# A first product of 20 products instead of 21, with its two halves overlapped, and the sums of x moved to the second product

## The chip, the cores and the metric

The kernel runs on one core of one Trainium2 chip. The metric is the device time of one execution in microseconds. A core has a matrix engine (PE in the profile), VectorE (DVE), ScalarE (ACT), GpSimd (POOL) and SyncE (SP, which here only issues DMAs). Each works through its own instructions in order and waits on semaphores for the others.

## The reference

A short causal convolution over tokens (7 taps, softmax weights, one set for each of 8 heads), then a two-layer network with a GELU in the form h·sigmoid(1.702 h), all in float32:

```python
# x (8, 4096, 192), weight (8, 7)
w = softmax(weight)                        # over the 7 taps
out = np.einsum('hk,bskhg->bshg', w, x_unf)   # x_unf: x and its 6 predecessors
x = out.reshape(32768, 192)
h = x @ w_in                               # (192, 2048)
g = h * (1.0 / (1.0 + np.exp(-1.702 * h)))
return g @ w_out                           # (2048, 192)
```

## The kernel before

All tokens are done in 32 steps ("big" 0 to 31) of 1024 tokens each; tokens lie along the free axis, features along the partitions. Every step has a convolution, a first product (w_in, and GELU on the way out of PSUM) and a second product (w_out). Step 0 is special (`first_step`), for the weights are still being unpacked then; the steady loop over `big` 1 to 31 stands at the end of the kernel function.

**First product.** The 192 features are 3 blocks of 64 (c = 0, 1, 2) and the tokens 2 blocks (n), so that x has six blocks; w_in has 4 by 3 blocks for each of two halves of its columns (v = 0, 1). The plain way takes 24 block products for each v. The kernel forms sums of blocks of w_in once (`SUMS_W`), and in each step sums of blocks of x (`SUMS_C`, eight of them), and takes 21 products of sums (`TERMS`, pairs of a sum of w_in and a sum of x), which it adds and subtracts into the eight outputs. A product (`product1`) is two matmuls of 64 rows, one for each row half of PE, and each writes one of the two PSUM banks of its slot; in float32 each matmul shows as two records, so a product is four records of 64 x 512. There are 4 pairs of banks: `slots[0]` to `slots[2]` and `sums`. `hidden(big, v, ...)` lists the order of a v half by hand: `pe` issues products, `copy2` (line 647, ACT) saves a pair of banks in a `room` place (k15 to k20), `sum2` (line 651, VectorE) adds or subtracts banks and places, `gelu` (lines 632 and 636, ACT) writes the rows of g. Between them `work` issues the convolution of block 1 (VectorE, `conv`), `taps_at` issues taps of the other blocks (ACT, `tap`), and `early` four groups of sums of the second product.

A product needs the same rows of x on both row halves, so each block and each sum is copied across the halves by DMA (`cross`, SP). `conv_t` has three parts: the own blocks and sums of even steps, the crossed ones, and the own ones of odd steps.

**Convolution.** Blocks 0 and 2 are made by taps: ACT multiplies by one weight (line 516) into a spare place, and either a DMA that accumulates (line 530, block 0, a small tree of sums) or GpSimd (line 518, block 2) adds up. Block 1 is made by VectorE, seven instructions (lines 502 and 504). The sums of x come from GpSimd (`sums_c`, lines 391 and 393; by VectorE in step 1), in the first product, through `prepare`.

**Second product.** Five by five blocks of g and w_out are again combined: `PLAN` is a list, written out, of main products (`main`), side products (`side`, on a fourth column strip of PE), sums of g (`sum`, VectorE, 128 x 1024), sums by an accumulating DMA (`acc`, issued by POOL), `seed` (ACT copies between places), `join` (VectorE), output transposes (`turn`) and stores. `("go", n)` issues n groups of four matmuls, three of the main product and one of the side; there are 78 groups of 0.433 us. A place of g is a `spot`, numbered 0 to 20; `("sum", 14, 14, "-", 18)` writes spot 14. Five sums (`EARLY_G`) are made by VectorE or DMA in the first product already. Spots that are no longer needed serve as places of the taps (`TAP_SPOTS`).

The engines are in order, and the program order is that of the lists (`manual_schedule`): an instruction that waits holds up all that stands behind it on its engine.

Of the kernel before, what the change touches and what calls it, by code (L numbers as in the profile page):

```python
# [8 lines left out]
F32 = mybir.dt.float32  # L9
# [6 lines left out]
def kernel(  # L16
# [8 lines left out]

# [41 lines left out]
    def load_x(big, ns=range(2)):  # L87
# [20 lines left out]
        [psum.tile([P, TOK], F32, name=f"slot{i}{h}") for h in range(2)] for i in range(3)  # L108
    ]
    sums = [psum.tile([P, TOK], F32, name=f"sums{h}") for h in range(2)]  # L110
# [17 lines left out]
    k15, k19, k20, k18, k16 = (room[:, i, :].rearrange("p (h n) -> p h n", h=2) for i in range(5))  # L128
# [17 lines left out]
    KEPT_LATE, TAP_SPOTS = 3, {0: (13, 16, 15), 2: (14, 17, 18), 3: (15, 16, 19)}  # L146

    def kept(i):
# [7 lines left out]
    NB = 13  # L156
    C11, C12, C21, C22, C31, C32, V2, V3, V4, V5, V6, V7, V8, V1 = range(NB + 1)
    conv_t = consts.tile([P, 3, NB, T], F32)
    SUMS_C = [
        (V1, C31, "-", C11),  # L160
        (V2, V1, "-", C32),
        (V3, C12, "+", V2),
        (V4, C22, "+", V2),
        (V5, C21, "-", V4),
        (V6, C11, "-", V5),
        (V7, C22, "-", C21),
        (V8, C32, "-", C22),
    ]

    def place(big, b):  # L170

        if b == V1:
            return V8 if big % 2 else C31
        return C31 if b == V8 and big % 2 else b

    def own(big):
        return conv_t[:, big % 2 * 2, :, :]
# [3 lines left out]
    NA = 21  # L181
    w_in_s = consts.tile([P, NA, UW], F32)
    SUMS_W = [
        (12, 10, "n", 11),
        (13, 12, "-", 2),
        (14, 3, "-", 12),
        (12, 1, "-", 13),
        (15, 4, "+", 13),
        (16, 3, "+", 5),
        (17, 2, "+", 5),  # L190
        (18, 0, "+", 3),
        (19, 6, "+", 8),
        (20, 19, "+", 10),
        (4, 4, "n", 16),
        (5, 2, "+", 11),
        (0, 0, "+", 2),
        (10, 7, "-", 10),
        (7, 7, "+", 19),
        (8, 8, "-", 11),
        (11, 9, "+", 11),  # L200
        (11, 11, "-", 19),
        (9, 9, "-", 3),
        (3, 3, "0", 3),
    ]

    TERMS = [
        (14, V2), (10, C21), (20, V5), (6, V3), (19, V6), (0, C11), (17, C32), (5, V8), (4, V7), (8, V1), (12, C22),
        (9, C12), (13, V4), (3, V3), (15, C22), (16, V6), (2, V1), (1, C21), (11, C11), (7, V7), (18, C12),
    ]

# [34 lines left out]
    assert PIECE == CW * D and 3 * PIECE <= NB * T and 3 * PIECE <= 2 * NJ * XW and 3 * PIECE <= FORMS * NG * HD  # L247
# [221 lines left out]
    def transpose_x(big, c, n=None):  # L469
# [14 lines left out]
        0: [conv_t[:, i, b : b + 2, :] for i in (1, 2) for b in (V2, V4, V6)],  # L484
# [23 lines left out]
    DMA_TAPS = (0,)  # L508
    TREE = {2: [(1, 2)], 4: [(3, 4)], 6: [(5, 6), (0, 1), (3, 5), (0, 3)]}
    TREE_1 = {2: [(1, 2)], 4: [(3, 4), (0, 1)], 6: [(5, 6), (0, 3), (0, 5)]}  # L510

    def tap(big, c, k):

        dst = own(big)[:, 2 * c : 2 * c + 2, :]
        home = tap_home(big, c, k) if k else dst
        act.mul(home, conv_src(big, c, k), cw[:, c, k : k + 1])  # L516
        if k and c not in DMA_TAPS and big > 1:
            nc.gpsimd.tensor_add(dst, dst, home)  # L518
            return
        homes = [dst] + [tap_home(big, c, i) for i in range(1, K)]  # L520
        for a, b in (TREE if big > 1 else TREE_1).get(k, ()):
            tree.append((homes[a], homes[b]))
        end_taps(2 if big == 2 and k == K - 1 else 0)

    tree = []

    def end_taps(left=0):
        while len(tree) > left:
            out, src = tree.pop(0)
            nc.gpsimd.dma_start(out=out, in_=src, accum_op=ALU.add)  # L530

    def sums_c(big, i):
        add_up(
            lambda j: own(big)[:, place(big, j), :],
            *SUMS_C[i],
            eng=vec if big == 1 else nc.gpsimd,
        )

    def cross(big, b0, b1):
        for o in range(2):  # L540
            nc.sync.dma_start(
                out=conv_t[halves[1 - o], 1, b0:b1, :], in_=own(big)[halves[o], b0:b1, :]
            )

    def copy_over(b):

        for o in range(2):
            act.copy(conv_t[halves[1 - o], 1, b, :], own(0)[halves[o], b, :])
# [3 lines left out]
    waiting = {True: [], False: []}  # L552
    given = {True: 0, False: -1}
    pieces = []

    def cross_now(early, big, b0, b1):
        if early or big == 1:
            cross(big, b0, b1)
        else:
            pieces.extend((big, b, min(b + 3, b1)) for b in range(b0, b1, 3))  # L560
# [5 lines left out]
    def cross_when(early, *what):  # L566
        if given[early] < what[0] - 1:
            waiting[early].append(what)
        else:
            cross_now(early, *what)  # L570

    def give(early, big):
        given[early] = big
        for what in waiting[early]:
            cross_now(early, *what)
        waiting[early].clear()

    def prepare(big):

        v1 = place(big, V1)  # L580
        def convs(*cs):
            for c in cs:
                for k in range(K):
                    yield "", 0.76 if k else 0.48, lambda c=c, k=k: conv(big, c, k)

        cost = 0.34 if big == 1 else 0.0
        yield from convs(1)
        yield f"conv {big}", 0.0, lambda: None
        yield f"done {big}", 0.0, lambda: need(f"taps {big}")
        yield "", cost, lambda: sums_c(big, 0)  # L590
        yield f"first {big}", 0.0, lambda: cross_when(True, big, v1, v1 + 1)
        yield "", 0.0, lambda: cross_when(False, big, 0, C31)
        for i in range(1, len(SUMS_C)):
            yield "", cost, lambda i=i: sums_c(big, i)
        rest = (C31, V8) if big % 2 else (C31 + 1, NB)
        yield f"all {big}", 0.0, lambda: cross_when(False, big, *rest)

    def prepare_taps(big):

        for c in (0, 2):  # L600
            for k in range(K):
                yield "", 1.0, lambda c=c, k=k: tap(big, c, k)
        yield f"taps {big}", 0.0, lambda: None

    def product1(slot, a, b, big, v, first=False):
        pair = conv_t[:, big % 2 : big % 2 + 2, place(big, b), :]
        for h in range(2):

            src = pair[halves[h], :, :] if h == big % 2 else pair[halves[h], ::-1, :]
# [9 lines left out]
    def terms(big, v, slot, *ts, first=False):  # L619
        for t in ts:  # L620
            product1(slot, *TERMS[t], big, v, first)
            first = False

    ALL = slice(0, TOK)

    def gelu(b, u, v, src):
# [3 lines left out]
        if isinstance(src, list):  # L630
            for h in range(2):
                act.activation(  # L632
                    dst[:, :, h, :], src[h].rearrange("p (o t) -> p o t", o=2), AF.Gelu_apprx_sigmoid
                )
        else:
# [3 lines left out]
                AF.Gelu_apprx_sigmoid,  # L639
            )  # L640
# [4 lines left out]
    def copy2(dst, src):  # L645
        for h in range(2):
            act.copy(bank(dst, h), bank(src, h))  # L647
# [10 lines left out]
    def hidden(big, v, x, z, y, sums, work, fetch, last=lambda: None):  # L658

        def pe(slot, *ts, first=False):
            terms(big, v, slot, *ts, first=first)

        def taps_at(n):
            for _ in range(0 if v else n):
                next_tap()

        def early(i):
            for item in (EARLY_G if big > 1 else EARLY_G_1)[i] if v else ():  # L670
                sum_g(*item)


        if v:
            pe(z, 7, first=True)
            give(True, big)
        if v:
            pe(sums, 12)
            copy2(k15, sums)
            pe(x, 5, 17)  # L680
        else:
            pe(x, 5)
            pe(sums, 12)
            copy2(k15, sums)
            pe(x, 17)
            taps_at(1)
        gelu(B11, 0, v, x)
        if not v:
            pe(z, 7, first=True)
        pe(sums, 0)  # L690
        copy2(k16, sums)
        taps_at(2)
        last()
        def turn_next():
            if big + 2 < N_BIG:
                need(f"done {big + 1}")
                turn_x(big + 2)

        early(0)
        if not v:  # L700
            work(2.0 if big > 1 else 1.6)
        elif big == 1:
            work(3.2)

        pe(y, 6, 14, first=True)
        sum2(vec.tensor_sub, x, z, k15)
        early(1)
        if not v or big == 1:
            work(1.6 if big > 1 else 1.2)
        pe(sums, 13)  # L710
        copy2(k19, sums)
        pe(x, 2)
        copy2(k18, x)
        taps_at(2)
        pe(z, 11)
        pe(sums, 20, 10)
        sum2(vec.tensor_sub, k15, y, k19)
        gelu(B12, 0, v, sums)
        pe(x, 4)
        copy2(k20, x)  # L720
        sum2(vec.tensor_sub, k19, z, k19)
        early(2)
        if not v or big == 1:
            work(1.1)
        gelu(B22, 1, v, k19)
        gelu(B22, 0, v, k15)
        taps_at(2)
# [565 lines left out]
```

## Time and profile before

| | |
|---|---|
| time, median of 3 runs | 2295.59 us (2294.99 to 2295.61) |
| profiled execution, span | 2294.0 us |
| busy: PE, VectorE, ACT, GpSimd | 2271.9, 1939.3, 1563.3, 843.7 us |
| matmuls of line 610, 64 x 512: records | 5400 (3740 into `slot`, 1660 into `sums`) |
| stages: first product of step 1 | 106.8 to 153.2 us |
| stages: step 12 | 887.5 to 923.8 (first), to 957.6 (second) |

The profile is of one execution. Its span runs from the first to the last instruction. A line of a group names the source line, the engine and the operation, what is written and read, the shape and the count, then the busy time, the mean length in ns, and the engine's idle time just before with what ended it. A window line gives for a stretch of time how long each engine was busy, and the number of instructions. A line that ends in `[0.40 <-PE sums L610]` says that the engine idled 0.40 us before it and what it waited for.

### The profile page before, as it was taken

What the parts mean: (1) busy time and instruction counts of PE and PEld (TensorE: products, weight loads), DVE (VectorE), ACT (ScalarE), POOL (GpSimd) and SP (SyncE); (2) the same over time, 40 slices, a digit from 0 to 9 for tenths busy, and PEclk for the clock granted to TensorE, in tenths of its full rate; (3) what the DMA queues carried; (4) which work ended last, traced back from release to release, by engine and by line L of the source; (5) the groups of instructions that cost most, each with busy time, mean ns of one, the idle gap of its engine ahead of it and who ended that gap; (6) DMA issues with size and microseconds to landing.
All of it is one profiled execution on the core that took longest, in us unless ns stands there. A gap on an engine that the chain in (4) does not pass through costs nothing.

```text
span 2294.0 us, 60960 instructions
## 1 busy us (share of the span) xinstructions
PE 2271.9 (99%) x25214; PEld 1206.9 (53%) x25214; DVE 1939.3 (85%) x2791; ACT 1563.3 (68%) x2968; POOL 843.7 (37%) x837
## 2 busy tenths in 40 slices
PE   9889999999999999999999999999999999999998
PEld 5355555555555555555555555555555555555556
DVE  8778888888888888888888888888888888888877
ACT  7567666677666776666776667776667766677754
POOL 1444433344424434333444234343334442344400
PEclk9899999999999999999999999999999999999999
DMA  8885666665666656666656656566666566564443
GB/s 196 149 158 117 117 125 136 128 125 113 126 133 125 138 113 117 125 136 128 127 113 127 134 123 139 113 115 125 139 127 128 113 127 135 122 140 86 91 98 70
DMA packets 270660, 286.56 MB, mean 125 GB/s; under 512 B 118064, under 2 KB 206128, under 8 KB 270256
## 3 DMA queue, kind: packets, MB, share of 16 engines
q0 software_dynamic: 58080, 151.48, 36.8%
q1 hardware_dynamic: 210656, 130.80, 25.4%
q8 instruction: 199, 3.26, 0.6%
q10 hardware_dynamic: 1648, 0.39, 0.1%
q14 instruction: 77, 0.63, 0.1%
HBM read 53.15 MB, written 25.17 MB: 34 GB/s over the span
## 4 chain that ended last, share of the span: by engine, by line
PE 94%; DMA 3%; DVE 1%; ACT 1%; POOL 0%; issue 0%; SPq 0%; POOLq 0%; ACTq 0%; DVEq 0%
PE slot L610 33%; PE slot L985 33%; PE sums L610 15%; PE sums L985 12%; DMA w_form<-w_form 1%; DMA g<-g 1%; DMA conv_t<-conv_t 0%; POOL w_form L437 0%; DMA conv_t<-w_form 0%; DMA w_out_s<-w_form 0%; DMA osbs<-in_moe_w_out_dram 0%; DVE xt L473 0%; DMA xin<-in_x_dram 0%; DVE conv_t L504 0%; ACT conv_t L1090 0%
## 5 line engine op out<-in xcount | busy, mean ns | idle before, releaser
L610 PE MATMUL slot<-conv_t,w_in_s 64*128 64x512 f32 x3740 | 861.6, 591 | 6.3 <-ACT room L647 6.0
L985 PE MATMUL slot<-g,w_form 128*32 128x256 f32 x7024 | 710.3, 379 | 0.0
L610 PEld LDWEIGHTS slot<-conv_t,w_in_s 64*128 64x128 f32 x3740 | 374.6, 187 | 432.7 <-issue 352.3
L393 DVE TENSOR_TENSOR g<-g 128x1024 f32<-128x1024 f32 x372 | 450.2, 1237 | 3.2
L985 PEld LDWEIGHTS slot<-g,w_form 128*32 128x32 f32 x7024 | 373.5, 110 | 119.7
L610 PE MATMUL sums<-conv_t,w_in_s 64*128 64x512 f32 x1660 | 407.9, 591 | 0.9 <-ACT room L647 0.6
L636 ACT ACTIVATE g<-room 128x1024 f32<-128x1024 f32 x310 | 325.7, 1077 | 67.1 <-DVE room L651 67.1
L1010 ACT COPY room<-slot 32x256 f32<-32x256 f32 x434 | 159.3, 367 | 310.4 <-PE slot L985 309.2
L985 PE MATMUL sums<-g,w_form 128*32 128x256 f32 x2648 | 368.8, 379 | 0.0
L985 PE MATMUL slot<-g,w_out_s 128*32 128x256 f32 x4080 | 318.8, 380 | 0.0
L961 POOL DMA_DIRECT2D g<-g x124 | 106.3, 858 | 499.2 <-PE sums L985 165.9
L610 PEld LDWEIGHTS sums<-conv_t,w_in_s 64*128 64x128 f32 x1660 | 172.0, 187 | 188.2 <-issue 141.4
L518 POOL TENSOR_TENSOR conv_t<-conv_t,g 128x512 f32<-128x512 f32 x180 | 260.5, 1447 | 14.3 <-POOL conv_t L518 3.0
L530 POOL DMA_DIRECT2D g<-g x120 | 104.3, 885 | 429.9 <-PE sums L985 119.5
L647 ACT COPY room<-slot 128x512 f32<-128x512 f32 x434 | 231.5, 601 | 40.8 <-PE slot L610 40.8
L516 ACT ACTIVATE g<-xt,cw 128x512 f32<-128x512 f32 x360 | 248.5, 730 | 2.2
L985 PEld LDWEIGHTS slot<-g,w_out_s 128*32 128x32 f32 x4080 | 164.7, 110 | 131.7 <-ACT g L632 22.7
L632 ACT ACTIVATE g<-slot 128x512 f32<-128x512 f32 x334 | 180.7, 598 | 45.1 <-PE slot L610 23.5
L985 PEld LDWEIGHTS sums<-g,w_form 128*32 128x32 f32 x2648 | 177.9, 110 | 36.7
L504 DVE SCALAR_TENSOR_TENSOR conv_t<-xt,cw,conv_t 128x512 f32<-128x512 f32 (+1 forms) x198 | 189.1, 955 | 4.6
L393 POOL TENSOR_TENSOR conv_t<-conv_t 128x256 f32<-128x256 f32 x180 | 182.2, 1026 | 9.4
L1010 ACT COPY room<-sums 32x256 f32<-32x256 f32 x217 | 79.6, 367 | 145.2 <-PE sums L985 142.5
(203 smaller groups left out, 2914.9 us busy)
## 6 DMA issues: line engine op xcount, KB each, us to landing
g<-g POOLq DMA_DIRECT2D x124, 512.0 KB, 5.6
xin<-in_x_dram SPq DMA_DIRECT2D x240, 180.0 KB, 4.4
conv_t<-conv_t SPq DMA_DIRECT2D x180, 192.0 KB, 3.2
g<-g POOLq DMA_DIRECT2D x120, 256.0 KB, 3.8
out_dram<-osbs SPq DMA_DIRECT2D x186, 128.0 KB, 5.0
g<-room POOLq DMA_DIRECT2D x31, 512.0 KB, 5.3
conv_t<-g POOLq DMA_DIRECT2D x60, 256.0 KB, 4.6
g<-osbs POOLq DMA_DIRECT2D x30, 512.0 KB, 4.7
```

Source lines behind the costliest of these rows:

```text
L393: eng.tensor_sub(v(dst), v(a), v(b))
L504: vec.scalar_tensor_tensor(out=dst, in0=src, scalar=tap, in1=dst, op0=ALU.mult, op1=ALU.add)
L516: act.mul(home, conv_src(big, c, k), cw[:, c, k : k + 1])
L518: nc.gpsimd.tensor_add(dst, dst, home)
L530: nc.gpsimd.dma_start(out=out, in_=src, accum_op=ALU.add)
L610: nc.tensor.matmul(slot[h], w_in_s[halves[h], a, v * P : (v + 1) * P], src, start=first, stop=True, skip_group_check=True,)
L632: act.activation(dst[:, :, h, :], src[h].rearrange("p (o t) -> p o t", o=2), AF.Gelu_apprx_sigmoid)
L636: act.activation(dst.rearrange("p o h t -> p h o t"), src.rearrange("p h (o t) -> p h o t", o=2), AF.Gelu_apprx_sigmoid,)
L647: act.copy(bank(dst, h), bank(src, h))
L961: nc.gpsimd.dma_start(out=spot(dst), in_=spot(a), accum_op=ALU.add)
L985: nc.tensor.matmul(dst, w, t, start=first, stop=last, skip_group_check=True)
L1010: act.copy(to, d)
```

## The change

- `SUMS_C` has eleven sums of five of the six blocks of x (block 4 is only in sums), `SUMS_W` 23 sums, `TERMS` 20 products. `slots` has all four pairs of banks, and `sums` is one of them.
- `FIRST` replaces the hand-written order: one list for a v half. Names a0 to a9 are pairs of banks, given out from a list `free` when first named and given back after the last use (`COUNT`); k0 to k6 are places in `room` (`ROOM_OF`). The first number of an item tells whose it is: 0 of this v half; 1 and 2 of the next one, so that eight of the 20 products of a half are done ahead. In v = 0 they are those of v = 1. In v = 1 the opening product (mark 2, the only one on block 2 of the six of x) is that of the next step; the items of mark 1 are put on `later`: the copies go out in the second product (`seeds_ahead`, at `final`), the rest at the start of the next first product (`rest_ahead`).
- `FILL` hangs other work on places of that list: twelve GpSimd adds of the convolution, three transposes of x, the early sums of g. `work` and taps are left there for step 1 alone (`FILL_1`).
- `conv_t` has the own blocks twice (by step), but one place for the eleven sums, one for their crossed copies and one for the crossed blocks, except the crossed block of the opening product, which has two. So the sums of the next step can be made only when the first product has been read: `vsum` items in `PLAN` (GpSimd), with `cross` items behind.
- Conv block 1 (c = 1) of steps from 3 on is made by taps on ACT too; GpSimd adds up blocks 1 and 2, and block 0 stays with the DMA tree (`tree` items). All 21 taps stand in `PLAN` (7 did before, at most one between two `go`; now up to four).

In the text, "P19" is the product of entry 19 of `TERMS`, counted from 0.

```diff
-    k15, k19, k20, k18, k16 = (room[:, i, :].rearrange("p (h n) -> p h n", h=2) for i in range(5))
+    rooms = [room[:, i, :].rearrange("p (h n) -> p h n", h=2) for i in range(5)]
...
-    KEPT_LATE, TAP_SPOTS = 3, {0: (13, 16, 15), 2: (14, 17, 18), 3: (15, 16, 19)}
+    KEPT_LATE, TAP_SPOTS = 3, {0: (11, 10, 16), 1: (17, 14, 20), 2: (15, 13, 9), 3: (15, 16, 19)}
...
-    conv_t = consts.tile([P, 3, NB, T], F32)
+    conv_t = consts.tile([P, 2 * NBLK + 2 * NV + len(REST) + 2, T], F32)
     SUMS_C = [
...
+        (6, 0, "-", 4), (7, 6, "-", 5), (8, 1, "+", 7), (9, 3, "+", 8), (10, 0, "-", 7), (11, 9, "-", 6),
+        (12, 2, "-", 10), (13, 2, "-", 4), (14, 13, "+", 11), (15, 0, "+", 14), (16, 14, "-", 1),
     ]
...
+    TERMS = [
+        (13, 9), (6, 14), (9, 0), (14, 5), (11, 6), (7, 2), (1, 3), (15, 3), (0, 0), (4, 16), (16, 8), (10, 2),
+        (17, 15), (18, 7), (2, 11), (8, 12), (3, 1), (12, 1), (5, 10), (19, 13),
+    ]
...
         if k and c not in DMA_TAPS and big > 1:
-            nc.gpsimd.tensor_add(dst, dst, home)
+            adds.append((dst, home))
+            if big == 2:
+                next_add()
             return
...
-    def hidden(big, v, x, z, y, sums, work, fetch, last=lambda: None):
...
+    FIRST = [
+        (0, "gelu", 2, 1, "a0", 1), (0, "prod", 14, "a1"), (0, "copy", "k0", "a2", 1),
+        (0, "sum", "a3", "a4", "-", "k1"), (0, "prod", 17, "a3"), (0, "sum", "a5", "k1", "-", "a1"),
+        (0, "prod", 3, "a4"), (0, "gelu", 3, 1, "a3", 1), (0, "prod", 16, "a5"), (0, "sum", "a6", "k0", "-", "a4"),
+        (0, "prod", 1, "a1"), (0, "gelu", 1, 0, "a5", 1), (0, "prod", 15, "a6"), (0, "prod", 7, "a4"),
+        (0, "copy", "a7", "a6", 1), (0, "gelu", 1, 1, "a4", 1), (0, "prod", 19, "a6"),
+        (0, "sum", "a8", "a1", "-", "k2"), (0, "prod", 5, "a7"), (0, "prod", 12, "a8"), (0, "copy", "k3", "a6", 1),
+        (0, "sum", "k4", "a8", "+", "k3"), (0, "gelu", 0, 1, "a7", 1), (2, "prod", 11, "a0"),
+        (1, "copy", "a2", "a0", 1), (0, "prod", 9, "a1"), (1, "prod", 0, "a2"), (1, "prod", 4, "a0"),
+        (0, "gelu", 2, 0, "k4", 1), (1, "copy", "k2", "a2", 1), (0, "prod", 8, "a8"),
+        (0, "sum", "a1", "a1", "+", "k3"), (1, "prod", 10, "a2"), (1, "copy", "k6", "a0", 1),
+        (0, "gelu", 0, 0, "a8", 1), (0, "sum", "k5", "a1", "-", "k0"), (1, "sum", "a4", "a2", "-", "k6"),
+        (1, "prod", 6, "a9"), (1, "prod", 2, "a0"), (1, "prod", 13, "a4"), (0, "gelu", 3, 0, "k5", -1),
+        (1, "copy", "k1", "a9", 1), (1, "prod", 18, "a2"),
+    ]
...
+    FILL = [
+        {
+            1: (("add", 4), ("add", 4), ("add", 4)), 9: (("turn", 0),), 15: (("turn", 1),), 21: (("turn", 2),),
+        },
+        {
+            3: (("g", 0),), 12: (("g", 1),), 17: (("g", 2),), 18: (("g", 3),), 31: (("g", 4),), 36: (("g", 5),),
+        },
+    ]
...
+    def hidden(big, v, now, nxt):
+
+        for i, (ahead, *item) in enumerate(FIRST):
+            for what in (FILL if big > 1 else FILL_1)[v].get(i, ()):
+                fill(big, *what)
+            if not ahead:
+                do(big, v, now, *item)
+            elif v == 0:
+                do(big, 1, nxt, *item)
+            elif nxt and ahead == 2:
+                do(big + 1, 0, nxt, *item)
+            elif nxt:
+                later.append(item)
...
     PLAN = [
...
+        ("side", 13, 16, "k0"), ("main", 1, 5, "p2", 1), ("vsum",), ("cross",), ("go", 3), ("vsum",), ("go", 1),
+        ("sum", 14, 14, "-", 18), ("main", 16, 10, "p3", 0), ("go", 2), ("sum", 7, 8, "-", 7), ("tap",), ("go", 1),
+        ("go", 1), ("main", 0, 14, "p0", 1), ("cross",), ("go", 1), ("sum", 5, 11, "-", 19), ("go", 1),
...
+        ("vsum",), ("go", 1), ("sum", 6, 8, "-", 6), ("go", 1), ("main", 5, 8, "p1", 0), ("go", 1),
+        ("sum", 4, 5, "-", 10), ("tap",), ("go", 1), ("seed", "k2", "p2", 1), ("tap",), ("go", 2),
+        ("sum", 0, 0, "+", 5), ("main", 14, 2, "p2", 0), ("go", 1), ("vsum",), ("go", 1), ("acc", 15, 4), ("go", 1),
+        ("join", "k3", "p1", "+", "k0"), ("vsum",), ("go", 1), ("sum", 11, 7, "+", 11), ("side", 11, 17, "k0"),
...
     for big in range(1, N_BIG):
         more = big + 1 < N_BIG
...
+        rest_ahead(big, half)
+        other = begin_half()
+        hidden(big, 0, half, other)
+        half = begin_half() if more else None
+        hidden(big, 1, other, half)
         if more:
-            need(f"all {big + 1}")
+            need(f"done {big + 1}")
+            cross_blocks(big + 1)
+            begin_sums(big + 1)
```

New functions that these call: `do` runs one item of `FIRST` (a product, a pair of copies, a pair of sums, a GELU); `begin_half` makes an empty table of names; `next_sum` issues one sum of x on GpSimd and, when a group of two or three is complete, puts its crossing on the list that `cross` takes from; `add_taps` issues one DMA of the tree; `next_add` issues one GpSimd add of the convolution.

More of the change, by code (lines that the diff above doesn't have):

```diff
@@ L183 @@
     SUMS_W = [
[L184 to L202, printed above, removed]
@@ L547, in copy_over @@
         for o in range(2):
[L548 to L560, printed above, removed]
+            act.copy(conv_t[halves[1 - o], cross_of(0, b), :], own(0)[halves[o], b, :])
+    pieces, sums_left = [], []
+    LAST_AT = {s[0]: i for i, s in enumerate(SUMS_C)}
+    ENDS = (NBLK, NBLK + 3, NBLK + 6, NB - 2, NB)
+    GROUPS = [range(*ends) for ends in zip(ENDS, ENDS[1:])]
     def cross_piece():
@@ new lines, in begin_sums, with done @@
+    def begin_sums(big):
+        sums_left.extend((big, i) for i in range(len(SUMS_C)))
+    def prepare(big):
+        for k in range(K if big < 3 else 0):
+            yield "", 0.76 if k else 0.48, lambda k=k: conv(big, 1, k)
+        yield f"conv {big}", 0.0, lambda: None
+        def done():
+            need(f"taps {big}")
+            while adds:
+                next_add()
+            if OPEN_SUM:
+                sums_c(big, *OPEN_SUM)
+            cross(big, OPEN, OPEN + 1)
+        yield f"done {big}", 0.0, done
@@ L617, in product1, with gelu @@
             )
[L619 to L622, printed above, removed]
     ALL = slice(0, TOK)
-    def gelu(b, u, v, src):
+    def gelu(b, u, v, src, sign=1):
         m, n = divmod(b, 2)
@@ new lines, with seeds_ahead, rest_ahead, plain @@
+    later = []
+    def seeds_ahead(big, half):
+        while later and later[0][0] == "copy":
+            dst = later[0][1]
+            if dst[0] == "a" and dst not in half[0] and not free:
+                return
+            do(big, 0, half, *later.pop(0))
+    def rest_ahead(big, half):
+        while later:
+            do(big, 0, half, *later.pop(0))
+    def plain(u, m, n, v, slot, ks=range(NC), first=0):
+        for k in ks:
+            product1(slot, NC * (2 * u + m) + k, 2 * k + n, 0, v, k == first)
@@ new lines, in fill @@
+    def fill(big, kind, *args):
+        if kind == "work":
+            work(*args)
+        elif kind == "tap":
+            next_tap()
+        elif kind == "add":
+            for _ in range(*args):
+                next_add()
+        elif kind == "turn":
+            need(f"done {big + 1}")
+            if big + 2 < N_BIG:
+                transpose_x(big + 2, *args)
+                if args[0] == NC - 1 and big + 3 < N_BIG:
+                    load_x(big + 3)
+        else:
+            sum_g(*(EARLY_G if big > 1 else EARLY_G_1)[args[0]])
@@ L1260, with final @@
             begin(big + 2)
-        second(big, x, y, sums, lambda: copy2(sums, z) if more else None, not more)
-        x, z = z, x
+        bx, bs, by = (free.pop(0) for _ in range(3))
+        def final():
+            free.append(bs)
+            if more:
+                seeds_ahead(big + 1, half)
+        second(big, bx, bs, by, final, not more)
+        free += [bx, by]
 _INS = ['x', 'weight', 'moe_w_in', 'moe_w_out']
```

362 lines of the change are left out of this document (174 added, 188 removed), and 56 rows, old and new, of tables (PLAN, SUMS_W).

## The prediction

> **What bounds the kernel now.** I read the busy times of the page first, then its chain of work that ended last, by engine.
>
> ```profile
> PE 2271.9 (99%) x25214; PEld 1206.9 (53%) x25214; DVE 1939.3 (85%) x2791; ACT 1563.3 (68%) x2968; POOL 843.7 (37%) x837
> ...
> PE 94%; DMA 3%; DVE 1%; ACT 1%; POOL 0%; issue 0%; SPq 0%; POOLq 0%; ACTq 0%; DVEq 0%
> ```
>
> The matmul engine is the chain. Next come sums over windows: one step of the steady loop, cut where the matmuls change from line 610 (first product) to line 985 (second product), then the second product cut once more at 20 us.
>
> ```profile
> core 0: us, PE busy (x) PEld busy (x) DVE busy (x) ACT busy (x) POOL busy (x), PEclk, DMA share, GB/s
> 887.54:923.79 36.25, 36.25 (x172) 16.70 (x168) 29.90 (x41) 30.39 (x51) 19.54 (x17) 1.00 0.59 117
> 923.79:957.60 33.81, 33.81 (x626) 20.17 (x625) 30.06 (x44) 18.20 (x42) 7.74 (x9) 1.00 0.67 135
> ...
> 923.79:943.79 20.00, 20.00 (x374) 12.10 (x376) 19.30 (x22) 8.81 (x23) 4.29 (x5) 1.00 0.88 183
> 943.79:957.60 13.81, 13.81 (x260) 8.07 (x252) 10.75 (x23) 9.39 (x19) 3.45 (x4) 1.00 0.37 66
> ```
>
> PE has no gap in the step, at full granted clock: 36.25 + 33.81 = 70.06 us. A matmul removed is time gained, and every new wait of PE is time lost. The third row shows the neighbour with least room: in the first 20 us of the second product VectorE is busy for 19.30. It works there through the 17 sums that PLAN interleaves with the matmuls that read them. Last the timeline of that step, for the prices (start, length, what, x how many), with two lines from 112 us, when PE comes out of a wait:
>
> ```profile
> 906.53 1.02 PE L610 MATMUL sums<-conv_t,w_in_s 64*128 64x512 f32 x4
> 907.39 1.88 PE L610 MATMUL slot<-conv_t,w_in_s 64*128 64x512 f32 x8
> 907.59 1.07 ACT L647 COPY room<-sums 128x512 f32<-128x512 f32 x2 [0.40 <-PE sums L610]
> ...
> 910.60 2.40 POOL L393 TENSOR_TENSOR conv_t<-conv_t 128x256 f32<-128x256 f32 x2
> 911.19 1.22 DVE L393 TENSOR_TENSOR osbs<-g 128x1024 f32<-128x1024 f32 x1
> 912.51 1.56 DVE L393 TENSOR_TENSOR osbs<-osbs,g 128x1024 f32<-128x1024 f32 x1
> ...
> 919.67 1.28 DVE L651 TENSOR_TENSOR room<-room,sums 128x512 f32<-128x512 f32 x2 [2.07 <-PE sums L610]
> ...
> 925.10 2.35 DVE L393 TENSOR_TENSOR g<-g 128x1024 f32<-128x1024 f32 x2
> ...
> 112.07 0.59 PE L610 MATMUL slot<-conv_t,w_in_s 64*128 64x512 f32 x1
> 112.12 0.59 PE L610 MATMUL sums<-conv_t,w_in_s 64*128 64x512 f32 x1
> ```
>
> To be seen: one product of the first kind is 4 records and 0.86 us, start to start (906.53 to 907.39). Its reader on ACT starts 0.20 us after that (907.59), and two copies of a bank each take 1.07. VectorE's pair of bank sums takes 1.28. A 1024-wide sum of VectorE takes 1.22, but 1.56 when GpSimd sums beside it: 0.35 more. At 112 us the two row halves of PE (one bank each) run out of step by 0.06 us, a new product beginning on one half while the other ends the old one.
>
> **The product removed.** Each of 31 steps has two v halves, so 62 products fall away: 62 x 0.86 = 53.2 us, or 1.72 a step. Left are 40 products, 34.32 us a step.
>
> **The new order of the first product.** Before, two products at least lie between a reader of a bank pair and the next product into that pair. After, in several places only one does: P15, copy a7<-a6, P7, P19 into a6; P11, copy a2<-a0, P9, P0 into a2 (for v=1, inside v=0); P0, copy k2, P4, P10 into a2 at the start of a step. The copies of the two banks end 0.20 + 0.59 = 0.79 and 0.20 + 1.07 = 1.27 us after the product; PE starts some 0.15 us later (my estimate: at 906.25 a weight load follows the copy that frees its bank by 0.05, and the first matmul of a step takes 693 ns against 589). Cover is 0.86. If the row halves may run out of step, as at 112 us, each waits for its own bank: 0.79 + 0.15 - 0.86 = 0.08, the second half staying 0.43 to 0.48 behind. If the pair goes as one, 1.27 + 0.15 - 0.86 = 0.56. A fourth place, the chain gelu(1,1), sum a8, P12, is late by about 0.1. I followed the list of FIRST down with these prices (ACT 0.48 a bank start to start, VectorE 0.60): waits of 0.09 to 0.14 at six or seven places, plus 0.43 of offset that is paid when the second product needs all rows, make 1.2 us a step; with pairs as one, 2.9. Least is the offset alone, 0.4. I take 1.2, since the 112 us lines show halves apart. Behind each such wait stands everything on PE, which is in order.
>
> By load, ACT has 28 bank copies and 24 bank gelus at 0.48 and four wide gelus at 0.96: 28.8 us of 34.3; VectorE 32 bank sums at 0.60, five 1024-wide at 1.13 and three transposes at 0.68: 26.9. Neither becomes the bound there.
>
> **VectorE's late start in the second product.** Its last work in the first product now hangs on P9: sum a1, sum k5, early sum 5, then PLAN's first sum (spot 14). P9 ends 1.29 us before the end (P8's 0.86 and the 0.43 of offset); 0.26 + 1.2 + 1.2 + 1.13 later is 2.5 us into the second product, against 1.31 before (925.10). Spot 14 is read after 8 of 78 groups of four matmuls, at 8 x 0.433 = 3.47; the sum ends at 3.72, so PE waits 0.4 with its answer time. Lateness against before: 1.2.
>
> **Sums of x moved beside VectorE's queue.** Eleven sums a step on GpSimd (eight before) leave the first product; nine stand in the first 45 of 78 groups. Two run before VectorE's first sum; seven meet it where it has no gap: 7 x 0.35 = 2.45 us. The first sums are needed early: in the trace of before, those of spots 8, 13, 6 and 15 end 1.0, 1.7, 1.5 and 1.2 us ahead of their matmuls, and VectorE idles once, 0.46 us, before 13. At spot 15 the lateness is 1.2 + 2.45 - 0.46 = 3.2 against 1.2: PE has lost 2.0 us by then, the 0.4 included. Least: the meetings cost nothing and only the 0.4 stays. Most: a whole 0.73 of GpSimd (its length alone) each, 7 x 0.73 = 5.1, so 4.6. I take 2.0, by the 1.56 row. Queued behind are the joins and out turns on VectorE, and POOL's accumulating DMAs, whose readers are 9 us or more away.
>
> The Trainium skill (SBUF — State Buffer, Who interferes with whom) says that a VectorE instruction with two SBUF inputs contends with a GpSimd one that reads SBUF, and that the loser blocks fully, for the whole instruction. The trace agrees that it costs, but with 0.35, not 0.73; by the rule at its worst the sum would take the 4.6.
>
> **Conv block 1 (c = 1) and the rest: nothing.** VectorE loses seven conv instructions a step (six at 0.99 on the group row of line 504, one at 0.44), which lay beside PE. ACT gains 14 taps in the second product, 14 x 0.62 = 8.7 on 18.2 busy of 33.8; side copies wait behind at most four taps, 2.5 us, where their banks come round after 8 groups, 3.5 us: if that cover failed, up to 1 us a step. GpSimd's twelve adds at 1.45 start near the first product and end 17.4 us later; gelu(0,1) of v=0 needs the sixth, at 8.7, some 6 us ahead. SP issues 4 more crossings a step, each landing in 3.2 us; the last is due over 10 us before its product. In the first two steps three more sums of w_in and three of x go to VectorE; 106.78 to 153.15 us already holds 10 us of waits: 0, from -3 to +8 in all.
>
> **Sum.** 31 x (1.2 - 1.72) = -16, and 30 x 2.0 = +60 (the last step has no sums of x): +44 on the profiled 2294.0, so 2338; the median of the runs is 1.6 above the profile: 2340 us.
>
> **Rivals.**
> - Faster: the moved sums cost VectorE nothing that reaches PE, because POOL slips into joins and gaps. For it: VectorE idles 3.1 us in the last 13.8 of the second product. Against: nine of eleven sums stand before that. Then 2295.6 - 53.2 + 31 x 0.4 = 2255 (2242 with no offset). Chance 0.27.
> - Even: waits of about 1.7 a step, each half of what I take; 2295. Chance 0.05.
> - Bank pairs go as one: 2.9 for 1.2 in the first product, 31 x 1.7 = 53 more, 2393. Against it the 112 us lines. Chance 0.12.
> - GpSimd's whole length blocks: 2.6 more on 30 steps, 2418. Against it the 1.56 row. This is the rule of the Trainium skill above. Chance 0.08.
>
> **How the numbers follow.** My forecast has the remaining 0.48 and a range of its own of 2305 to 2375: meetings at 0.25 to 0.40 each, PE's answer 0.05 to 0.25. From 2254 to 2395 about half of the faster case lies out below and the worst cases above, 2 in 10 together. Within 0.2% (2291 to 2300), about what a measurement here tells from no change, lies the even case: faster 0.27, same 0.05, slower 0.68.
>
> **What would show it.** In the profile after: 5152 records of the first product's matmul line for 5400, with row halves 0.4 us out of step; first products near 35.5 us; second products of 35.5 to 36 us, with PE waiting on a VectorE sum about 8, 16 and 42 to 48 groups in, and many 1024-wide sums at 1.56. I am wrong if second products still take 33.8 us, if PE's waits there end on ACT or a DMA, or if first products pass 37 us.

## The result and the profile after

The changed kernel takes 2383.38 us (median of 4 runs, 2382.92 to 2385.3), the kernel before 2295.35 (2294.99 to 2295.61): ratio 1.0386, 95% interval 1.0371 to 1.04. It is slower by 88 us; the forecast was 2340 (2305 to 2375), slower by 44.

First the page of the changed kernel: busy times, the chain by engine, and the group of VectorE's 1024-wide sums (372 of them, mean 1408 ns; 1237 before).

```profile
PE 2285.4 (96%) x24966; PEld 1353.0 (57%) x24966; DVE 2049.1 (86%) x2842; ACT 1779.4 (75%) x3481; POOL 1133.5 (48%) x1101
...
PE 49%; DVE 35%; issue 7%; ACT 5%; DMA 4%; SPq 1%; POOL 0%; DVEq 0%; ACTq 0%; POOLq 0%
...
L363 DVE TENSOR_TENSOR g<-g 128x1024 f32<-128x1024 f32 x372 | 514.2, 1408 | 8.5 <-DMA g<-osbs 3.3
```

PE fell from 99% busy to 96%, and a third of the chain of waits, 35%, is now VectorE, where it was 1%. Next the sums over windows of one steady step: the first product (line 595, once 610), the second (line 1010, once 985), and the second cut at 20 us. After each window's length come the busy times.

```profile
core 0: us, PE busy (x) PEld busy (x) DVE busy (x) ACT busy (x) POOL busy (x), PEclk, DMA share, GB/s
1065.76:1101.45 35.69, 35.69 (x160) 22.05 (x161) 27.48 (x42) 29.16 (x54) 18.02 (x16) 1.00 0.43 89
1101.45:1138.52 37.07, 34.81 (x625) 20.26 (x625) 35.76 (x45) 26.69 (x57) 18.45 (x20) 1.00 0.82 164
1101.45:1121.45 20.00, 18.18 (x333) 10.81 (x336) 19.86 (x17) 10.68 (x26) 9.20 (x11) 1.00 0.81 174
1121.45:1138.52 17.07, 16.63 (x300) 9.45 (x292) 15.90 (x29) 16.01 (x32) 9.25 (x9) 1.00 0.83 152
```

The first product became shorter, 36.25 to 35.69. The second became longer, 33.81 to 37.07, and in its first 20 us VectorE has no gap left (19.86 of 20.00). The view of waits says what PE waited for in that second product (in all, times, longest):

```profile
PE slot L1010 <- DVE g L363: 1.8, 1, 1.8
PE slot L1010 <- DVE room L363: 0.4, 1, 0.4
```

Start to start of the groups of four matmuls, PE loses 2.03 us at group 35 (the sum of spot 5), 0.72 at group 43 (the sum of spot 6 and the join behind it, which frees the bank p4), 0.27 at group 61 (a join) and 0.18 at the end, where the kernel before loses 0.11. The first two make 2.75 of the 3.26 us by which the second product grew.

Over the whole run: 29 steady steps x (35.69 - 36.25) = -16.2, 29 x (37.07 - 33.81) = +94.5; in 7 of these steps the second product is 0.7 to 1.2 longer still, which with small differences of the others makes +8.1; step 0 +1.3, step 1 +0.9 (41.49 + 39.55 against 46.37 + 33.81), the last step -0.6. The sum is +88.0; the two profiled spans, 2381.9 and 2294.0, lie 87.9 apart.

Why VectorE is late shows in the timeline of both engines in that step (start, length). Six lines are VectorE's, then come GpSimd's.

```profile
1105.91 4.03 DVE L363 TENSOR_TENSOR g<-g 128x1024 f32<-128x1024 f32 x3
1109.86 1.75 DVE L363 TENSOR_TENSOR room<-g 128x1024 f32<-128x1024 f32 x1
1111.53 1.21 DVE L361 TENSOR_TENSOR osbs<-osbs,g 128x1024 f32<-128x1024 f32 x1
1112.67 0.41 DVE L361 TENSOR_TENSOR room<-slot,room 96x256 f32<-96x256 f32 x1
1113.00 2.31 DVE L361 TENSOR_TENSOR g<-g 128x1024 f32<-128x1024 f32 x1
1115.24 5.11 DVE L363 TENSOR_TENSOR g<-g 128x1024 f32<-128x1024 f32 x3
...
1107.77 2.75 POOL L361 TENSOR_TENSOR conv_t<-conv_t 128x256 f32<-128x256 f32 x2
1112.51 1.71 POOL L363 TENSOR_TENSOR conv_t<-conv_t 128x256 f32<-128x256 f32 x2
1115.62 0.87 POOL L986 DMA_DIRECT2D g<-g  x1 [1.39 <-DVE g L361]
1116.22 1.70 POOL L363 TENSOR_TENSOR conv_t<-conv_t 128x256 f32<-128x256 f32 x2
```

The sum at 1113.00 takes 2.31 us. GpSimd's pair ends at 1112.51 + 1.71 = 1114.22, and the sum 1.09 us after that, nearly its own length alone (1.22): it ends as if it had stood still until both GpSimd sums were done. This is no single case: in the whole trace 89 stretched 1024-wide sums of VectorE end 1.08 or 1.09 us behind the GpSimd sum or series beside them, and 29 joins 0.28 or 0.29. The pairs come from GpSimd's queue: two sums of x wait together behind an accumulating DMA, then run one after the other. Only sums that stand ready like this keep VectorE out. In the pair at 1107.77 the second sum starts 0.08 us after the first has ended; VectorE's sum gets in between, and GpSimd's pair takes 2.75. Over seven traces (before, after, x3 to x7) a VectorE sum or join that was held up got in at 225 of 229 places where two GpSimd sums lie some 0.1 apart, and at none of 343 where their records overlap by some 0.2 to 0.6.

### The profile page after: what moved, and what is told of

The parts are those of the page before. It is cut to its first block, busy times and chain, and to the rows that moved or that the text cites. A ratio compares the mean times of both kernels' runs of the same rounds, so it can differ in the third digit from the quotient of the medians.

```text
span 2381.9 us, 62150 instructions
## 1 busy us (share of the span) xinstructions
PE 2285.4 (96%) x24966; PEld 1353.0 (57%) x24966; DVE 2049.1 (86%) x2842; ACT 1779.4 (75%) x3481; POOL 1133.5 (48%) x1101
## 4 chain that ended last, share of the span: by engine, by line
PE 49%; DVE 35%; issue 7%; ACT 5%; DMA 4%; SPq 1%; POOL 0%; DVEq 0%; ACTq 0%; POOLq 0%
PE slot L595 37%; DVE g L363 16%; PE slot L1010 11%; DVE g L361 7%; DVE room L363 3%; DVE room L361 2%; DVE osbs L361 2%; ACT g L612 2%; DVE slot L636 2%; DVE room L636 1%; ACT g L617 1%; DMA conv_t<-conv_t 1%; DMA g<-osbs 1%; ACT slot L630 1%; DMA g<-g 1%
## 5 line engine op out<-in xcount | busy, mean ns | idle before, releaser
L595 PE MATMUL slot<-conv_t,w_in_s 64*128 64x512 f32 x5152 | 1154.4, 597 | 4.6 <-ACT room L630 2.3
L595 PEld LDWEIGHTS slot<-conv_t,w_in_s 64*128 64x128 f32 x5152 | 699.6, 186 | 448.4 <-issue 221.5
L1010 PE MATMUL slot<-g,w_form 128*32 128x256 f32 x9672 | 920.4, 380 | 11.4 <-DVE room L363 10.5
L363 DVE TENSOR_TENSOR g<-g 128x1024 f32<-128x1024 f32 x372 | 514.2, 1408 | 8.5 <-DMA g<-osbs 3.3
L636 DVE TENSOR_TENSOR slot<-slot,room 128x512 f32<-128x512 f32 x496 | 321.9, 694 | 220.5 <-ACT g L612 118.8
L612 ACT ACTIVATE g<-slot 128x512 f32<-128x512 f32 x776 | 429.3, 610 | 75.3 <-PE slot L595 75.1
L504 POOL TENSOR_TENSOR conv_t<-conv_t,g 128x512 f32<-128x512 f32 x354 | 461.9, 1308 | 23.1
L363 POOL TENSOR_TENSOR conv_t<-conv_t 128x256 f32<-128x256 f32 x210 | 258.8, 1297 | 2.4
L1010 PE MATMUL slot<-osbs,w_form 128*32 128x256 f32 x2232 | 228.8, 379 | 0.0
L361 POOL TENSOR_TENSOR conv_t<-conv_t 128x256 f32<-128x256 f32 x120 | 185.5, 1545 | 2.4
L636 DVE TENSOR_TENSOR slot<-room,slot 128x512 f32<-128x512 f32 x248 | 159.5, 689 | 27.3 <-PE slot L595 25.2
L636 DVE TENSOR_TENSOR room<-slot,room 128x512 f32<-128x512 f32 x248 | 159.2, 683 | 5.3 <-ACT room L630 2.1
```

The lines of the kernel that those rows point to most:

```text
L361: eng.tensor_add(v(dst), v(a), v(b))
L363: eng.tensor_sub(v(dst), v(a), v(b))
L595: nc.tensor.matmul(slot[h], w_in_s[halves[h], a, v * P : (v + 1) * P], src, start=first, stop=True, skip_group_check=True,)
L612: act.activation(dst[:, :, h, :], src[h].rearrange("p (o t) -> p o t", o=2), AF.Gelu_apprx_sigmoid, scale=float(sign),)
L636: op(*(bank(t, h) for t in (dst, a, b)))
L1010: nc.tensor.matmul(dst, w, t, start=first, stop=last, skip_group_check=True)
```

## The experiments

Theory: GpSimd's sums of x, now in the second product, hold up VectorE's sums, which PE needs. Rivals: ACT's added taps, the new order of the first product, VectorE's late start. "Second product" below is the length in most steady steps; each ratio, with its 95% interval, is against the kernel before.

### Without the sums, and without their reads

```diff
 def next_sum():
-    sums_c(big, *SUMS_C[i])
+    if big == 1:
+        sums_c(big, *SUMS_C[i])
+    else:
+        nc.gpsimd.memset(conv_t[:, slot_of(big, SUMS_C[i][0]), :], 0.0)
```

x2 is this; x1 has no `else`.

> Leaves out GpSimd's eleven sums of x of every step after the first (their values stay those of the first step); crossings, waits and the order on every other engine stay. Contention theory (GpSimd's sums hold up VectorE's sums in the second product): second products fall from 37.1 to 33.8-34.3 us, the 1024-wide VectorE sums from a mean of 1408 to about 1240 ns, total 2280-2297 us. Rival (ACT's taps or the new order of the first product cause the loss): second products stay at 37 us, total near 2383 us. Late-start theory (VectorE's first sum comes late whatever GpSimd does): a wait of 0.4 us or more stays, total about 2305 us.

> Each of those GpSimd sums becomes a GpSimd memset of the same place, so GpSimd works at the same points and waits for the same things but reads nothing; the values of the sums are left out. If what holds VectorE is GpSimd's reading of SBUF: second products 33.8-34.3 us, total 2280-2297 us, as without the sums. If it is any work of GpSimd there, its writes, or its waits and signals: second products stay between 35.5 and 37.1 us, total above 2330 us.

Measured: x1 2318.94 us (1.0102, 1.0082 to 1.0122), second products 34.6 at best, median 35.0. x2 2309.24 us (1.0060, 1.004 to 1.008), second products 34.63. Both fell most of the way, and both missed the expected 2280 to 2297. Timeline of x2, the same two sums, then GpSimd:

```profile
1149.03 0.41 DVE L361 TENSOR_TENSOR room<-slot,room 96x256 f32<-96x256 f32 x1
1149.36 1.21 DVE L361 TENSOR_TENSOR g<-g 128x1024 f32<-128x1024 f32 x1
...
1148.81 0.89 POOL L559 MEMSET conv_t<- 128x256 f32 x2
```

The 2.31 is 1.21 again, though GpSimd works at the same places, with the same waits and writes: it is its reads that hold VectorE up. A memset is shorter than a sum (0.89 for two against 1.71), but that is not the reason: over the whole trace the sums and joins of VectorE without a PSUM input that overlap work of GpSimd are 2 us longer than alone in x2, in all, and 149 us in the changed kernel. Reads cost 37.07 - 34.63 = 2.44 us a step. But 0.82 over 33.81 stays, more than I had expected: 0.38 at group 61, 0.3 at the start of the next first product, the rest in pieces of 0.02. No wait of 0.4 is at group 8: the first PLAN sum ends 0.06 before PE needs it, so the late start by itself costs nothing. In x1's longer steps the wait at group 61 is larger; in the one followed back, a tap had stood 0.75 us behind a DMA, and ACT's copies behind the tap.

### Fewer taps

```diff
 for c, k in order:
-    yield "", 1.0, lambda c=c, k=k: tap(big, c, k)
+    if big < 3 or c != 1 or k == 0:
+        yield "", 1.0, lambda c=c, k=k: tap(big, c, k)
```

> Leaves out taps 1 to 6 of conv block 1 from step 3 on, and GpSimd's adds of them (twelve ACT halves fewer in the second product, six GpSimd adds fewer in the first). Contention theory: second products stay near 37.1 us, at most 0.4 us less (the wait at group 61, which in the kernel without GpSimd's reads ends on a VectorE join that had waited for ACT's copies behind five taps); total 2365-2383 us. Rival (ACT's added taps cause the loss): second products fall below 35 us, total below 2315 us.

Measured: 2380.91 us (1.037, 1.0351 to 1.0389), second products 36.98. ACT's taps are not the main cause. This does not show that they cost nothing: a wait that they cause is hidden while VectorE is late anyway.

### Copies in the other order

```diff
 def copy2(dst, src, sign=1):
-    for h in range(2):
+    for h in (1, 0):
```

> The whole computation; each pair of bank copies in the first product does the bank of the second row half first, so that the row half that is ahead waits longest. If the row halves of PE run out of step and each waits for its own bank: the offset is taken away or turned round, and first products rise from 35.7 to about 37.2-37.4 us, total about 2430-2436 us. If the halves do not matter (pairs go as one in any case): first products stay at 35.7 us, total 2383 us.

Measured: 2500.66 us (1.0894, 1.0872 to 1.0916), first products 38.61, second 38.14. The waits of PE in one of those first products:

```profile
PE slot L595 <- ACT slot L630: 1.0, 3, 0.4
PE slot L595 <- issue: 0.5, 1, 0.5
PE slot L595 <- ACT room L630: 0.3, 1, 0.3
```

PE now waits for copies, of which the same view of the changed kernel has no line: the order of the banks is worth 2.9 us a step there (38.61 - 35.69), of which the view shows 1.8 as waits. In the second product the waits for VectorE's sums grow from 1.8 to 3.2 us by the view of waits, and it is 1.1 longer. The direction came as expected, the size did not (I had 1.5 to 1.7 and nothing in the second product).

### The sums at other places of the second product

x3 puts three sums at the start of PLAN and eight behind trees 2 to 5; x6 puts the eight behind tree 4; x7 is x6 with two taps moved from groups 52 and 55 to 62 and 64.

The core of x6:

```diff
 PLAN = [
+    ("vsum",), ("cross",), ("vsum",), ("vsum",),
...
     ("sum", 6, 6, "-", 17), ("main", 10, 14, "p0", 0), ("go", 1), ("tree",),
+    ("vsum",), ("vsum",), ("vsum",), ("cross",), ("vsum",), ("vsum",), ("vsum",), ("cross",),
+    ("vsum",), ("vsum",), ("cross",),
```

> The whole computation, with the eleven GpSimd sums of x at other places of PLAN: three at the start of the second product, before VectorE's first sum, and eight after VectorE's last early sum (behind the fourth accumulating DMA), with their crossings. Contention theory (the loss is GpSimd's sums in the stretch where VectorE's sums are late for PE): second products 33.9-34.6 us, total 2283-2305 us. If the sums cost the same wherever they stand beside VectorE: second products 36.5-37 us, total above 2365 us. If the late start of VectorE costs by itself: a wait of 0.4 us or more at one of the first sums, total about 2300-2310 us.

> The whole computation: three GpSimd sums of x at the start of PLAN, the other eight behind its fourth tree DMA, which goes out when VectorE's last 1024-wide sum of PLAN has ended (25.8 us against 24.2 us into the second product in the kernel without GpSimd's reads); crossings right behind. What the previous placing showed (a VectorE sum of 5.01 us beside four GpSimd sums in a row, and a wait of 2.2 us at group 61) says that a GpSimd sum must not stand before the last of these. Contention theory: second products 34.3-35.0 us, of which 0.4 us is the wait at group 61; total 2290-2310 us. If GpSimd's sums cost the same beside the joins and turns that VectorE does there: 35.5-37 us, total above 2330 us.

> As the kernel with the eight sums behind the fourth tree DMA, and two of ACT's taps of conv blocks 2 and 1 moved from groups 52 and 55 to groups 62 and 64. If the wait at group 61 comes from ACT's copies behind the taps: it goes, second products 34.1-34.5 us, total 2275-2292 us, faster than before. If it comes from VectorE alone: it stays, as in the kernel with the taps in place.

Measured: x3 2393.35 us (1.0426, 1.0408 to 1.0443), second products 37.7 in the median, up to 39.4; x6 2339.29 (1.0189, 1.017 to 1.0207), 34.7, but more than 35.5 in eleven of 29 steps, up to 39.3; x7 2334.97 (1.017, 1.0156 to 1.0184), 35.39. x3 missed: slower than the changed kernel. One VectorE sum had stood beside a series of GpSimd sums (the first line). x6 missed too: its total is that of its rival, above 2330, though most steps are as short as expected. There it is a join that stands beside a series; the other lines are of its worst step, with GpSimd's below:

```profile
1132.12 5.01 DVE L363 TENSOR_TENSOR g<-g 128x1024 f32<-128x1024 f32 x1
```

```profile
963.88 4.32 DVE L361 TENSOR_TENSOR room<-room 96x256 f32<-96x256 f32 x1 [1.01 <-ACT room L1035]
968.12 0.42 DVE L361 TENSOR_TENSOR slot<-slot,room 96x256 f32<-96x256 f32 x1
...
964.14 1.06 POOL L361 TENSOR_TENSOR conv_t<-conv_t 128x256 f32<-128x256 f32 x1
964.84 3.07 POOL L363 TENSOR_TENSOR conv_t<-conv_t 128x256 f32<-128x256 f32 x4
```

The join, 0.41 us alone, took 4.32: it ends at 968.20, 0.29 after the fifth GpSimd sum in a row (964.84 + 3.07 = 967.91). In x3 a 1024-wide sum took 5.01. Fewer meetings are no help where the sums come in series. The view of waits puts PE's wait down to the join into a PSUM bank (968.12), which had only stood behind the held one. x7's moved taps did not take the wait at group 61 away (0.34), and pushed work of ACT into the next step's start; that expectation missed too.

### The sums in the first product

```diff
-    3: (("g", 0),), 12: (("g", 1),), 17: (("g", 2),), 18: (("g", 3),), 31: (("g", 4),), 36: (("g", 5),),
+    0: (("vsum", 5),), 2: (("vsum", 1),), 3: (("g", 0),), 12: (("g", 1),), 13: (("vsum", 1),),
+    17: (("g", 2), ("vsum", 1)), 18: (("g", 3),), 31: (("g", 4),), 36: (("g", 5),), 37: (("vsum", 3),),
...
+        elif kind == "vsum":
...
+            for _ in range(*args):
+                next_sum()
```

x8 is this, the second table of `FILL`, with no ("vsum",) in PLAN and seven ("cross",) at groups 0 to 24 there. x9 spreads the taps of groups 42 to 69 over groups 37 to 69. x10 mends one place of x9 (below), lets PLAN's sums of spots 5 and 7 change places, and issues step 1's sums of x in the second product, as the changed kernel does. x11 adds four ("cross",), at groups 30, 36, 45 and 59.

> The whole computation: GpSimd's sums of x leave the second product altogether. Each is put into the second half of the first product, behind the last product that reads its place (five at once, then one, one and one, and three behind the early accumulating DMA), where VectorE mostly sums banks of PSUM; the crossings stay at the start of the second product. Theory (only VectorE instructions with two SBUF operands are held up by GpSimd's sums): second products 34.6 us as in the kernel without GpSimd's reads, first products 35.7 us, total 2305-2315 us. If GpSimd's sums hold up VectorE's bank sums too: first products rise by 1 us or more, total above 2340 us.

> As the kernel with the sums in the first product, and ACT's taps from group 42 on spread: two go out at groups 37 and 39, the others singly or in pairs up to group 69, so that ACT's copies wait behind two taps at most. If the wait of 0.38 us at group 61 and the 0.3 us at the end of the second product come from ACT's copies behind taps: second products 33.9-34.3 us, total 2285-2297 us. If they come from VectorE's joins alone: unchanged at 34.6 us.

> The whole computation, as the kernel with the sums in the first product and the taps spread, with three edits: the tap at group 18 stands behind the seed copy again (it stood before it, and PE waited 0.64 us for that copy at group 19); VectorE's PLAN sums of spots 5 and 7 change places, so that the one that waits for the early accumulating DMA comes later; and step 1 issues its GpSimd sums where the changed kernel does. If the waits of the second product come from VectorE held up by GpSimd and from ACT's copies behind taps, and from nothing else: second products 33.9-34.1 us, first products 35.7 us, total 2283-2294 us, as fast as before or faster. If another wait takes their place: 34.5 us or more, total above 2300 us.

> The whole computation, as the kernel with the seed copy first, with four more places in PLAN from which a crossing may go out (groups 30, 36, 45 and 59). They serve step 1 alone, whose later crossings had gone out behind the stores, so that PE waited 8.1 us for them at the start of step 2; in all other steps there is nothing left to cross there. If that wait was the cause of step 1's 90.6 us: step 1 takes 82-84 us and step 2's first product 35.7, the steady steps stay at 69.7 us, total 2286-2292 us, 0.2 to 0.4% below before. If step 1 only shifts its waits: total stays near 2299 us.

Measured:

| | us | ratio (95%) | first, second product |
|---|---|---|---|
| x8 | 2312.66 | 1.0072 (1.0059 to 1.0086) | 35.69, 34.66 |
| x9 | 2308.18 | 1.0056 (1.0043 to 1.0068) | 35.72, 34.60 |
| x10 | 2299.41 | 1.0021 (1.0011 to 1.003) | 35.72, 34.00 |
| x11 | 2291.07 | 0.9985 (0.9976 to 0.9994) | 35.72, 34.04 |

Timeline of x8 in the first product, VectorE, then GpSimd:

```profile
1063.79 1.29 DVE L636 TENSOR_TENSOR slot<-room,slot 128x512 f32<-128x512 f32 x2
1065.51 1.29 DVE L636 TENSOR_TENSOR slot<-room,slot 128x512 f32<-128x512 f32 x2 [0.42 <-PE slot L595]
...
1063.46 1.53 POOL L361 TENSOR_TENSOR conv_t<-conv_t 128x256 f32<-128x256 f32 x2
1064.95 1.41 POOL L363 TENSOR_TENSOR conv_t<-conv_t 128x256 f32<-128x256 f32 x2
```

Four GpSimd sums in a row lie beside bank sums, one of whose operands is in PSUM ("slot"), and these take 1.29 a pair, as ever. First products keep 35.69, and second products are those of x2 with the whole computation done. The same work of GpSimd is free here and costs 2.4 us a step in the second product.

Most of the remaining 0.85 is ACT's. Groups of VectorE's instructions, x8 and then x11 (busy, mean ns, then idle time before them and what ended it):

```profile
L361 DVE TENSOR_TENSOR room<-room 96x256 f32<-96x256 f32 x155 | 87.7, 566 | 38.2 <-ACT room L1042 37.1
```

```profile
L361 DVE TENSOR_TENSOR room<-room 96x256 f32<-96x256 f32 x155 | 76.1, 491 | 1.8 <-ACT room L1043 0.3
```

In x8 joins wait 37 us in all for a copy that ACT has queued behind taps; in x11, with the taps spread, 0.3. x9's second products fell by only 0.06, and its expectation missed: the waits at group 61 and at the end were gone, but I had put a tap ahead of a seed copy, and PE waited 0.64 for that at group 19. x10 puts it back: 34.00. Its step 1 took 90.6 us, though, which put its total over the expected 2283 to 2294: its late crossings had gone out behind the stores (PE waited 8.1 us for them); x11's four places mend that. In x11 a steady step is 35.72 + 34.04 = 69.76 us against 70.06 before, with no wait in the second product worth a line:

```profile
1062.72:1096.76 34.04, 34.04 (x626) 19.69 (x625) 30.88 (x45) 27.16 (x57) 11.46 (x14) 1.00 0.85 166
1096.76:1132.48 35.72, 35.72 (x165) 21.96 (x161) 28.41 (x43) 28.85 (x54) 22.54 (x23) 1.00 0.46 99
```

x11 is 0.15% faster than the kernel before. The 29 steady steps give 6.9 us (0.3 in most of them, less in some), step 0 and the last step 1.5; step 1 takes 3.2 back (43.81 + 39.60 against 80.18). It is the only version here below before, and by less than the 0.2% that I called telling; its interval excludes 1.

## Why the prediction was right in direction and half in size

- Product removed and new order of the first product: -0.52 a step forecast (1.2 - 1.72), -0.56 measured; -16 forecast, -16.2 measured. This was no luck: in the step above the row halves start 0.44 us apart (1065.76 and 1066.20), and each half loses another 0.8, most of it in six or seven places of about 0.1, as forecast. x4 shows what the other order of banks costs.
- VectorE's late start: 0.4 forecast at group 8, nothing measured there. The first PLAN sum starts 2.19 us into the second product, not 2.5, and ends 0.06 ahead of its use. It is 0.88 later than before (1.31), not 1.2, and this still counts further on, where the meetings have used up VectorE's lead.
- **The step that failed is a size: "seven meet it where it has no gap: 7 x 0.35 = 2.45 us".** Against x2, four VectorE sums of the step above are longer, by 0.42, 0.53, 1.10 and 1.42: 3.47 in all up to the sum of spot 15, which ends that much later (23.42 us into the second product against 19.92). Fewer meetings, but two of them cost more than a whole GpSimd sum (0.73), since a VectorE sum waits until GpSimd's series ends. The forecast's way of adding up holds: with the measured terms it reads 0.88 + 3.47 - 0.46 = 3.89 at spot 15 against a lead of 1.2, so 2.7, and PE has lost 2.75 by group 44, where 2.0 was forecast. I took the price from one row, 1.56, and did not read it to its end: there GpSimd's pair ended at 910.60 + 2.40 = 913.00, 0.49 after the VectorE sum's start at 912.51, and the sum 1.07 after that. It was a short meeting under the same rule, not a price for every meeting; and I left out that the change makes pairs, two sums behind one accumulating DMA. The rival "GpSimd's whole length blocks" had the mechanism, with more meetings than there are: its 2418 is 35 off on the other side, my 2340 43. In the Trainium skill (SBUF — State Buffer, Summary: rules for kernel authors) the second one to issue "fully blocks" until the first finishes; these traces agree that it blocks, but behind a whole series (4.32 us beside five sums) and not behind one instruction. By the same page (Who interferes with whom) a GpSimd instruction that only writes, or a VectorE one with one SBUF input, does not contend: x2 and x8 agree (1.21 and 1.29).
- PE's waits: forecast at groups 8, 16 and 42 to 48, measured at 35 and 43. The lead of VectorE's sums over their use is 0.06 us for the first and differs from sum to sum, and it ran out at spot 5: before, that sum ended 13.19 us into the second product, 2.4 ahead of group 36 (36 x 0.433 = 15.59), and 0.88 + 3.47 - 2.4 = 1.95 of the 2.03 follow.
- **Conv block 1: "nothing".** Right in the total of the changed kernel (x5: 2380.91), but only because VectorE's lateness hid it; wrong by itself: 34.66 to 34.04 with the taps spread, 0.6 a step. The cover that I named (banks of the side copies, 3.5 us against 2.5) held; a join that needs such a copy, behind up to five taps, did not.
- The 7 longer steps, most of 8.1 us, were in no term. In four of them VectorE's sum of spot 7 waits 0.7 to 1.0 for the early accumulating DMA, and PE 1.6 at group 15; x8 still has three such steps, of 35.6 to 36.0, and in x10, where the sum changes places with its neighbour, none is above 34.53. The other three lose their time elsewhere, at groups 19 and 42 to 61, and why stays open.
- First two steps: 0 (-3 to +8) forecast, +2.1 measured.

So of the 44 us missing in the forecast, 29 x (3.26 - 2.0) = 36.5 are the second product's steady loss and 8.1 those steps; the small rest cancels. Of the 1.26 a step, about 0.75 came up to group 44, by the size of the meetings, and 0.5 behind it, where the forecast had nothing. The experiments share the 3.26 out by what each removal gives in their order, for a wait that is taken away uncovers the next: GpSimd's reads 2.44 (x2), then ACT's taps some 0.6 (x8 to x11), and 0.2 stays.

## What to carry to other kernels

Before work moves to GpSimd, look at what VectorE does at the same time: beside instructions with a PSUM operand GpSimd's sums cost nothing here, beside SBUF-only ones a VectorE instruction waits for all that GpSimd has ready in a row. Price a meeting by the series that the queue will form, not by one row of the old trace. And a cause that an experiment shows to be free may only stand behind a larger one: take the larger away and measure again.

## What was not expected of the hardware

- One VectorE join of 0.41 us took 4.32 beside five GpSimd sums in a row, a 1024-wide sum 5.01. GpSimd waits for VectorE too: the pair at 1107.77, where VectorE got in between, took 2.75, against 0.73 for one sum alone.
- GpSimd's memsets at the same places (0.89 for two) cost VectorE nothing.
- A long wait of PE can have an aftermath. In x6's worst step the granted clock, full until then, is 0.66 and 0.58 in the stretches behind a wait of 3.2 us, and three groups take 0.85 instead of 0.43:

```profile
964.80:967.60 2.80, 0.77 (x16) 0.20 (x8) 2.80 (x1) 2.78 (x6) 2.80 (x5) 1.00 1.11 186
967.60:969.30 1.70, 0.70 (x8) 0.40 (x12) 1.67 (x4) 1.20 (x3) 1.54 (x3) 0.66 1.13 193
969.30:972.00 2.70, 2.70 (x32) 1.23 (x28) 2.05 (x5) 0.00 (x0) 2.04 (x3) 0.58 0.92 261
```

It was so behind four of x6's five gaps of 3.2 to 3.4 us between matmuls; behind the one that ends at 1328.3 us the clock stays at 1.00. Behind the wait of 2.03 us at group 35 of the changed kernel the next groups took 0.43.
